# Maxout of a fused recurrent-attention and maxout-FFN kernel: evacuated by one ScalarE copy and two VectorE maxima of PSUM and SBUF

## The chip, the cores and the metric

One core of a Trainium2 chip. The metric is the device time of one execution in microseconds (us), the median of several. A run is called slow where it is over 1.5% above the fastest of its kernel, which here comes with a lower granted TensorE clock; ratios and verdicts use fast runs alone, while a median quoted without a further word is that of all runs, slow ones included. The profile's span is about 2 us shorter than the time, because it starts with the first recorded instruction. Engines: PE is TensorE, PEld its weight loads, DVE is VectorE, ACT is ScalarE, POOL is GpSimd, SP is the queue that issues the loads and stores.

## The reference, cut to what matters

```python
# attention: 4 batches, 8 heads, 768 positions, head size 48, a recurrence with decay alpha
state = alpha[:, :, t, :, None] * state + einsum('bhd,bhe->bhde', k[:, :, t], v[:, :, t])
y[:, :, t] = einsum('bhd,bhde->bhe', q[:, :, t], state)
# x: y as 3072 tokens x 384;  w1, w2, w3: 384 x 768;  w_out: 768 x 384
h = np.maximum(np.maximum(x @ w1, x @ w2), x @ w3)
out = h @ w_out
```

## The kernel before

The work is cut into 12 steps, each 128 positions of two batches (u = 0, 1). A step's pieces have one letter each, and hand-written strings fix in which order they are emitted; each engine runs its own part of that order strictly in turn. N takes logs of alpha, D multiplies by decays (matmul, two exponentials on ACT, then the k and q products), T transposes the products on PE and copies them out of PSUM, A makes and masks the scores, Y attends, X transposes y back into xT, M makes the decay factors of the state from D's third exponential, S updates the state, V scales v, G makes one gate tile, O projects. A gate pass has nine tiles: three groups of 256 columns by three weights. H is a run of matmuls on zeros that only keep PE's clock up. W casts a third of the gate weights (the last W: the output weights) on POOL. PSUM banks go round in rings: T, D and A share two banks ("w"), the gates have four.

```python
eng = nc.vector if s < 3 else nc.gpsimd
nc.gpsimd.tensor_mul(kv, raws[s, "k"][:, hs], ic)   # two SBUF inputs, fp32
eng.tensor_mul(qv, raws[s, "q"][:, hs], ac)
# ... T
nc.vector.tensor_copy(out=qkT, in_=tps)             # PSUM -> SBUF
# ... X
nc.vector.tensor_copy(out=xT.rearrange("p f u t -> p u f t"), in_=xtp_of.pop(s))
# ... gate: g is the weight (0, 1, 2), jg the group
if g < 2:
    h_of[g] = work.tile([P, 2, U * P], FP16, name=f"h{g}", tag=f"h{g}")
    nc.scalar.copy(out=h_of[g], in_=gps)
else:
    nc.vector.tensor_max(h_of[0], h_of[0], h_of[1])                             # two SBUF inputs
    nc.vector.tensor_max(hT_of[s][:, 2 * jg:2 * jg + 2, :], gps, h_of[0])       # PSUM and SBUF

STEADY = """T0 S0 N0 G0 G1 D0 T1 S1 O1 A0 G2 G3 O0 A1 G4 Y0 G5 Y1 X0 G6 D1 X1 G7 V0 G8 M0"""
```

## Time and profile before

| | before |
|---|---|
| median of 3 runs | 176.11 us |
| busy PE / DVE / ACT / POOL | 90% / 67% / 62% / 33% of a span of 174.4 us |
| one steady step (six of them alike) | 12.82 us, PE busy 12.04 |
| first gate matmul | at 31.34 us |
| PE waits for the copy qkT | 6 times, 4.7 us |

Read it from the engine that is never long without work. From the first gate matmul to the end PE is busy almost throughout, so a change pays only where it closes a hole of PE or lets the gates begin earlier. The lines that show this stand in the prediction below.

### The profile page before, as it was taken

Reading aid. Unit: us, or ns where it says so; the run is one execution under the profiler, and the core shown is the slowest. Engines: PE = TensorE matmul, PEld = TensorE weight load, DVE = VectorE, ACT = ScalarE, POOL = GpSimd, SP = SyncE. Lnnn points to the kernel's source line nnn. Section 1 sums busy time; section 2 is a strip of 40 time slices with the busy share of each in tenths; the row PEclk is TensorE's granted clock in tenths of the full one; section 3 lists DMA queues with packets and bytes.
Section 4 is the critical chain, followed back from the end, with each engine's and each line's share of the span. In section 5 each row is a group of like instructions: output and inputs, shape, how many; then the busy total and the mean of one; then the engine's idle time right before and its main releaser. Section 6 shows DMA issues by size and latency. Waiting matters only on the chain.

```text
span 174.4 us, 4372 instructions
## 1 busy us (share of the span) xinstructions
PE 156.9 (90%) x1762; PEld 120.2 (69%) x1762; DVE 116.1 (67%) x191; ACT 108.4 (62%) x205; POOL 57.1 (33%) x78
## 2 busy tenths in 40 slices
PE   7946788999999999989989999899899899899991
PEld 2324455799876777857867768778668768769870
DVE  4085769874646758588587687786777776776530
ACT  2627553466869775946946946946936937636551
POOL 0303128755191570540540540540540540500000
PEclk9995558999999999999999999999999999999999
DMA  6999999997999999998995955956951011011013
GB/s 132 220 218 218 170 243 325 358 347 157 180 230 219 180 294 213 222 218 200 218 217 117 225 125 116 204 137 136 182 137 51 0 45 49 0 49 45 0 49 135
DMA packets 107253, 28.70 MB, mean 165 GB/s; under 512 B 99809, under 2 KB 107233, under 8 KB 107233
## 3 DMA queue, kind: packets, MB, share of 16 engines
q1 hardware_dynamic: 106944, 28.32, 74.7%
q8 instruction: 14, 0.23, 0.6%
q10 hardware_dynamic: 288, 0.10, 0.3%
q14 instruction: 7, 0.05, 0.1%
HBM read 23.69 MB, written 4.72 MB: 163 GB/s over the span
## 4 chain that ended last, share of the span: by engine, by line
PE 78%; DVE 10%; ACT 4%; DMA 3%; issue 2%; SPq 1%; ACTq 0%; DVEq 0%
PE ops L282 14%; PE tps L179 6%; DVE qkT L183 4%; DVE lat L196 4%; DMA rq<-in_q_dram 3%; PE yps L210 2%; PE lps L146 2%; PE xtp L222 2%; PE yps L207 2%; PE wps L293 2%; PE sps L250 2%; PE sps L247 1%; SPq L85 1%; ACT xb L214 1%; PE lps L149 1%
## 5 line engine op out<-in xcount | busy, mean ns | idle before, releaser
L268 PEld LDWEIGHTS <-wcat 128*128 128x128 f16 x648 | 59.8, 98 | 8.7 <-issue 0.3
L282 PE MATMUL ops<-wo_97,hT 128*128 128x384 f16 x144 | 27.0, 326 | 0.6 <-DVE st_1_93 L254 0.6
L285 ACT COPY ob<-ops 128x384 f32<-128x384 f32 x24 | 11.6, 482 | 16.8 <-PE ops L282 16.8
L214 ACT ACTIVATE xb<-yps,c_69 128x384 f16<-128x384 f32 x24 | 14.0, 583 | 8.5 <-PE yps L210 8.4
L282 PEld LDWEIGHTS <-hT 128*128 128x128 f16 x144 | 13.6, 98 | 7.5 <-issue 0.7
L183 DVE COPY qkT<-tps 128x1024 f16<-128x1024 f16 x24 | 16.3, 686 | 2.6 <-PE tps L179 2.5
L155 ACT ACTIVATE ic<-lps,c_69 128x384 f32<-128x384 f32 x24 | 14.4, 599 | 2.3 <-PE lps L146 2.3
L156 ACT ACTIVATE ac<-lps,c_69 128x384 f32<-128x384 f32 x24 | 14.3, 597 | 0.0
L159 POOL TENSOR_TENSOR qk_86<-rk,ic 128x384 f16<-128x384 f32 x6 | 6.3, 1053 | 23.4 <-ACT ic L155 23.4
L193 PEld LDWEIGHTS <-qkT 48*128 48x128 f16 x192 | 6.1, 97 | 11.0 <-issue 7.5
L159 POOL TENSOR_TENSOR qk_85<-rk,ic 128x384 f16<-128x384 f32 x6 | 6.0, 998 | 22.3 <-ACT ic L155 16.4
L159 POOL TENSOR_TENSOR qk_87<-rk,ic 128x384 f16<-128x384 f32 x6 | 6.0, 1000 | 22.1 <-ACT ic L155 22.1
L159 POOL TENSOR_TENSOR qk_84<-rk,ic 128x384 f16<-128x384 f32 x6 | 6.0, 1001 | 20.8 <-ACT ic L155 20.8
L210 PE MATMUL yps<-vt,lat 128*128 128x48 f16 x192 | 11.8, 188 | 0.1
L170 ACT ACTIVATE vt<-rv,c_69 128x768 f16<-128x768 f32 x12 | 11.5, 957 | 0.0
L225 DVE COPY xT<-xtp 128x768 f16<-128x768 f16 x12 | 6.7, 556 | 7.0 <-PE xtp L222 7.0
L293 PE MATMUL wps<-blank 128*128 128x512 f16 x26 | 10.2, 553 | 1.2 <-DVE blank L340 1.2
L210 PEld LDWEIGHTS <-lat 128*128 128x128 f16 x192 | 10.2, 100 | 0.7 <-DVE lat L196 0.3
L222 PE MATMUL xtp<-c_68,xb 128*128 128x128 f16 x72 | 8.4, 228 | 1.0 <-ACT xb L214 0.8
L207 PEld LDWEIGHTS <-qkT 128*128 128x128 f16 x80 | 7.6, 96 | 0.2
L293 PEld LDWEIGHTS <-blank 128*128 128x128 f16 x26 | 3.1, 130 | 5.2 <-issue 3.3
L179 PE MATMUL tps<-c_68,qk_85 128*128 128x128 f16 x48 | 4.5, 248 | 2.3 <-DVE qkT L183 1.6
(442 smaller groups left out, 376.1 us busy)
## 6 DMA issues: line engine op xcount, KB each, us to landing
ra<-in_alpha_dram SPq DMA_DIRECT2D x12, 384.0 KB, 4.6
rk<-in_k_dram SPq DMA_DIRECT2D x12, 384.0 KB, 5.6
rq<-in_q_dram SPq DMA_DIRECT2D x12, 384.0 KB, 5.9
rv<-in_v_dram SPq DMA_DIRECT2D x12, 384.0 KB, 5.8
out_dram<-ob SPq DMA_DIRECT2D x24, 192.0 KB, 2.1
ws_0_114<-in_moe_w_dram SPq DMA_DIRECT2D x1, 384.0 KB, 5.2
ws_1_116<-in_moe_w_dram SPq DMA_DIRECT2D x1, 384.0 KB, 4.7
ws_2_118<-in_moe_w_dram SPq DMA_DIRECT2D x1, 384.0 KB, 5.6
```

What stands on the lines that cost most here:

```text
L155: nc.scalar.activation(out=ic, in_=lv, func=AFT.Exp, bias=nat_c, scale=-1.0)
L156: nc.scalar.activation(out=ac, in_=lv, func=AFT.Exp, bias=at_c)
L159: nc.gpsimd.tensor_mul(kv, raws[s, "k"][:, hs], ic)
L179: nc.tensor.transpose(tps[:, i, p, :], qk[:, i, u * HP + p].rearrange("p a b -> p (a b)"), ident)
L183: nc.vector.tensor_copy(out=qkT, in_=tps)
L210: nc.tensor.matmul(yps[:, p, i, :], lat[:, i, p, :], vt[:, u * H + 2 * p + i, :], start=(cb == 0), stop=(cb == 0 or i == 1))
L214: nc.scalar.mul(xb, yps.rearrange("p a b d -> p (a b d)"), ys_c)
L222: nc.tensor.transpose(xtp[:, u, f, :], xb[:, f * P:(f + 1) * P], ident)
L268: nc.tensor.matmul(gps[:, j, :], wcat[:, f, g, jj * P:(jj + 1) * P], xT[:, f].rearrange("p u t -> p (u t)"), start=(f == 0), stop=(f == NF ...
L282: nc.tensor.matmul(ops, hT_of[s][:, jj, u * P:(u + 1) * P], wo16[:, jj, :], start=(jj == 0), stop=(jj == NJ - 1))
L285: nc.scalar.copy(out=ob, in_=ops)
L293: nc.tensor.matmul(wps, blank[:, :P], blank, start=True, stop=True)
```

## The change

The intent: leave VectorE no instruction with two SBUF inputs in the steady part, so that it cannot collide there with GpSimd's products. ScalarE copies only the first of three gate tiles, VectorE takes two maxima of a PSUM tile and an SBUF tile, ScalarE takes over the copy of xT, and in the opening (the first three steps) the k product goes to VectorE. The order strings were set anew.

```diff
-        nc.gpsimd.tensor_mul(kv, raws[s, "k"][:, hs], ic)
+        eng.tensor_mul(kv, raws[s, "k"][:, hs], ic)
...
-            nc.vector.tensor_copy(out=xT.rearrange("p f u t -> p u f t"), in_=xtp_of.pop(s))
+            nc.scalar.copy(out=xT.rearrange("p f u t -> p u f t"), in_=xtp_of.pop(s))
...
-            h_of[g] = work.tile([P, 2, U * P], FP16, name=f"h{g}", tag=f"h{g}")
-            nc.scalar.copy(out=h_of[g], in_=gps)
+            h = work.tile([P, 2, U * P], FP16, name=f"h{g}", tag=f"h{g}")
         else:
-            nc.vector.tensor_max(h_of[0], h_of[0], h_of[1])
-            nc.vector.tensor_max(hT_of[s][:, 2 * jg:2 * jg + 2, :], gps, h_of[0])
+            h = hT_of[s][:, 2 * jg:2 * jg + 2, :]
+        if g == 0:
+            nc.scalar.copy(out=h, in_=gps)
+        else:
+            nc.vector.tensor_max(h, gps, h_of[g - 1])
+        h_of[g] = h
...
     PROLOGUE: (cut)  H8 -> H9; H5 ahead of T0@2 gone (H0); W0 from behind S1@0 to ahead of D0@2
-    STEADY = """T0 S0 N0 G0 G1 D0 T1 S1 O1 A0 G2 G3 O0 A1 G4 Y0 G5 Y1 X0 G6 D1 X1 G7 V0 G8 M0"""
+    STEADY = """N0 T0 S0 T1 G0 G1 D0 S1 O1 A0 O0 G2 A1 G3 Y0 G4 D1 G5 Y1 G6 X0 X1 G7 M0 V0 G8"""
     (cut: FIRST, SECOND and LAST are reordered too)
```

More of the change, by code (lines that the diff above doesn't have):

```diff
@@ L321, in emit @@
                 fn(step, int(piece[1:]))
-    PROLOGUE = """N0@0 H11@0 D0@0 D1@0 N0@1 H8@0 V0@0 T0@0 T1@0 A0@0 A1@0 D0@1 Y0@0 D1@1 X0@0 Y1@0
-        T0@1 H2@0 A0@1 T1@1 N0@2 V0@1 A1@1 X1@0 Y0@1 D0@2 D1@2 X0@1 H5@0 T0@2 Y1@1 M0@0 T1@2
-        S0@0 V0@2 A0@2 S1@0 W0 X1@1 A1@2 W1 W2 W3"""
-    FIRST = """G0@0 G1@0 G2@0 G0@1 G1@1 G2@1 Y0@2 G3@0 G4@0 G5@0 G3@1 G4@1 Y1@2 X0@2 G5@1 G6@0 G7@0
+    PROLOGUE = """N0@0 H11@0 D0@0 D1@0 H9@0 N0@1 V0@0 T0@0 T1@0 A0@0 A1@0 D0@1 Y0@0 D1@1 T0@1 N0@2
+        H2@0 X0@0 A0@1 Y1@0 T1@1 V0@1 Y0@1 A1@1 X1@0 X0@1 W0 D0@2 D1@2 T0@2 Y1@1 T1@2 X1@1
+        H0@0 A0@2 V0@2 M0@0 S0@0 S1@0 W1 W2 A1@2 W3"""
+    FIRST = """G0@0 G1@0 Y0@2 G2@0 G0@1 G1@1 G2@1 G3@0 G4@0 X0@2 G5@0 G3@1 G4@1 G5@1 G6@0 G7@0 Y1@2
         G8@0 G6@1 X1@2 G7@1 G8@1"""
-    SECOND = """N0@3 G0 G1 G2 D0@3 D1@3 M0@1 G3 G4 O0@0 G5 T0 O1@0 G6 N0 S0 O0@1 A0 V0@3 G7 T1 D0 S1
-        O1@1 A1 G8 Y0 Y1 D1 M0 X0 V0 X1"""
-    STEADY = """T0 S0 N0 G0 G1 D0 T1 S1 O1 A0 G2 G3 O0 A1 G4 Y0 G5 Y1 X0 G6 D1 X1 G7 V0 G8 M0"""
-    LAST = """G0 G1 G2 G3 G4 G5 O0 G6 G7 G8 O1"""
+    SECOND = """N0@3 G0 G1 G2 D0@3 D1@3 G3 O0@0 N0 G4 G5 T0 G6 M0@1 V0@3 S0 O1@0 A0 O0@1 G7 T1 D0 S1
+        O1@1 A1 Y0 D1 Y1 X0 M0 G8 X1 V0"""
+    STEADY = """N0 T0 S0 T1 G0 G1 D0 S1 O1 A0 O0 G2 A1 G3 Y0 G4 D1 G5 Y1 G6 X0 X1 G7 M0 V0 G8"""
+    LAST = """G0 G1 G2 G3 G4 G5 G6 G7 O1 G8 O0"""
     load(1)
```

## The prediction

> **What bounds the kernel now.** I read the page's busy shares first (PE 90%, DVE 67%, ACT 62%, POOL 33%), then the busy time of each engine stretch by stretch, then the waits of PE, and last the instructions in order of time around one wait. The loop's steps repeat every 12.82 us, so I cut the stretches at the steps (each starts at the first transposes of a step). The columns: stretch, its length, then busy us (and instructions) of PE, PEld, DVE, ACT, POOL; granted clock; DMA share; GB/s.
>
> ```profile
> 59.58:71.97 12.39, 12.28 (x154) 9.88 (x152) 8.05 (x14) 9.25 (x20) 4.95 (x7) 1.00 0.94 215
> 84.79:97.61 12.82, 12.04 (x151) 9.63 (x149) 9.46 (x15) 8.77 (x18) 4.47 (x7) 1.00 0.88 186
> 136.07:148.90 12.83, 12.05 (x152) 9.65 (x150) 9.45 (x15) 8.78 (x18) 4.49 (x7) 1.00 0.09 32
> 148.90:160.40 11.50, 10.87 (x134) 8.61 (x132) 9.36 (x15) 6.07 (x11) 1.86 (x4) 1.00 0.10 36
> ```
>
> PE works 12.04 us of each 12.82, at full clock and whatever the DMA does (share 0.88 or 0.09, same step). PE is the bound, with one hole of 0.78 us a step. The waits of PE name the hole (us in total, times, longest); from 35 to 60 us and from 160 us on PE waits for nothing:
>
> ```profile
> PE tps L179 <- DVE qkT L183: 4.7, 6, 0.8
> PE ops L282 <- DVE st_1_93 L254: 0.6, 1, 0.6
> ```
>
> The hole in order of time (start, duration, what):
>
> ```profile
> 119.90 0.43 DVE L275 TENSOR_TENSOR h_2102<-h_2102,h_2134 128x512 f16<-128x512 f16 x1
> ...
> 122.59 1.00 POOL L159 TENSOR_TENSOR qk_85<-rk,ic 128x384 f16<-128x384 f32 x1 [6.84 <-ACT ic L155]
> 123.55 1.01 POOL L160 TENSOR_TENSOR qk_85<-rq,ac 128x384 f16<-128x384 f32 x1
> 123.57 1.27 DVE L275 TENSOR_TENSOR h_2186<-h_2186,h_2218 128x512 f16<-128x512 f16 x1 [1.03 <-ACT h_2218 L273]
> 124.94 0.69 DVE L276 TENSOR_TENSOR hT<-gps_2222,h_2186 128x512 f16<-128x512 f32 x1
> 125.55 0.68 DVE L183 COPY qkT<-tps 128x1024 f16<-128x1024 f16 x1
> 126.28 0.61 PE L179 MATMUL tps<-c_68,qk_85 128*128 128x128 f16 x8 [0.78 <-DVE qkT L183]
> ```
>
> The same maximum of two SBUF tiles takes 0.43 us at 119.90, with POOL idle, and 1.27 us at 123.57, beside a POOL product that runs until 124.56: 0.84 us too much. The maximum of PSUM and SBUF behind it starts late, the copy of the transposes starts late, and PE's second group of transposes waits for that copy (it needs the bank) 0.78 us. So the hole is the lock, carried through three VectorE instructions.
>
> **What the Trainium skill says.** "SBUF — State Buffer", section "SBUF: two separate sides": VectorE and GpSimd share a port pair under an exclusive lock; an instruction of VectorE with two SBUF inputs takes part against a GpSimd one that reads SBUF, and the loser blocks for the whole instruction. The trace agrees (0.43 against 1.27 us). "TensorE: Matmul & The Clock Gate", Part 1: the array's clock is halved until an activity window of about 3.4 us was busy. The trace agrees in the opening: eight transposes took 1.01 us at 20.49 and 0.45 us from start to next from 27.9 on. "VectorE: DVE Perf Modes", section "The perf-mode tier table": an elementwise VectorE instruction of two tensors gets 2x for 16-bit SBUF operands and 1x with a PSUM operand. The trace agrees: 0.42 against 0.69 us for 512 columns.
>
> **The change part by part.**
>
> 1. Maxout. Before, per group of three gate tiles: two ScalarE copies (587 ns) and, on VectorE, 0.42 us (SBUF with SBUF) and 0.69 us (PSUM with SBUF). After: one copy and two of 0.69 us. Three groups a step. ScalarE: 3 x 0.59 = 1.8 us less. VectorE: 3 x (0.69 - 0.42) = 0.8 us more, minus the 0.84 us of lock.
>
> 2. The copy of xT goes from VectorE (0.56 us) to ScalarE. Estimate for 768 columns on ScalarE: the copies took 482 ns for 384 and 587 for 512 columns, 0.82 ns a column, so 482 + 384 x 0.82 = 0.80 us. ScalarE ends at about 8.8 - 1.8 + 0.8 = 7.8 us a step, VectorE at 9.45 + 0.8 - 0.84 - 0.56 = 8.9 us. Neither nears 12.04.
>
> 3. No VectorE instruction of the steady part has two SBUF inputs any more, so the lock has nothing to meet. POOL is as before.
>
> 4. New orders. I walked one steady step with the durations above, PE being in order: T 0.44, S 0.34, T 0.44, two gates of 0.66, D 0.16, S 0.34, O 0.97, A 0.43, O 0.97, and so on. The tight places: the first A needs the exponentials of D out of its bank. D starts at 2.53, its result is there at 2.9, the two exponentials end at 3.97, A's second bank is asked for at 4.0: just in time. The second A (6.06) needs the second masked product of the first one (ends about 5.7). X1 (10.40) needs the scaled copy that ends at about 10.35. The second T needs T1's bank, free since D1's exponentials (9.6 of the step before). No hole is left, but three margins are under 0.4 us; I charge 0.05 us a step. Steps 4 to 9: 6 x 0.78 = 4.7 us. Step 10: the 0.63 us wait for the state (its stretch shows 11.50 - 10.87). Step 3 (12.39 against 12.04): 0.3 us. Together 5.6, minus 8 x 0.05 = 0.4: **5.2 us gained** between 59 and 160 us.
>
> 5. The opening. For the first three steps the k product goes to VectorE too. Two products together took 2.25 us on both engines when they locked each other (25.33 to 27.58), and four in a row on VectorE at 0.65 us are 2.6 us, but the first pair is ready after 1.3. Followed through the opening's chain (products, transposes, copy, scores, mask, twice per step) this makes each of the three rounds 0.4 to 0.6 us later on VectorE, not cumulatively, because the next round waits for its own data and banks. Five warming matmuls (2.34 us at 25.07) are gone just ahead of the third round, and the clock had come back in them; without them PE may be at half clock until 30 or 34 us. The gates began at 31.34; from there PE was busy without a hole up to 60. By my walk they begin at 31.9 to 32.6, with up to 2 us of gates at half clock. Against that, the counts of warming matmuls were plainly set with care (9 and 0 where 8 and 5 stood), so I take less than the walk: **1.2 us lost**. The weights don't bind: their last cast ended at 38.95, and the gates that need it came at 41.5.
>
> 6. The second step's order puts the last scores, two attends and D1 close together: an attend comes about 1.2 us after scores whose two masked products need about 1.5. I charge **0.4 us lost**. The last step and the tail (18 output matmuls, one copy, one DMA) are as before: 0.
>
> Sum: -5.2 + 1.2 + 0.4 = -3.6. From 176.1: **172.5**; I lean a little further, to **172.3**, since the skipped holes in the opening (PE was busy 26.9 of the first 35 us) leave room for the reordering to win something.
>
> **The rivals.**
>
> A. Nothing fills: another wait takes the hole's place. For it: VectorE stays at 8.9 of 12 us in strict order, and margins of 0.03 to 0.4 us stand at the scores and at X1. Against it: VectorE and ScalarE both lose work, and the walk finds no wait above 0.1 us. If half the hole comes back (0.4 us a step), the time is 175.
>
> B. The clock in the opening. For it: granted clock 0.5 in the slices from 13 to 26 us, and the gap where the five matmuls stood. Against it: other pieces moved forward into 20 to 24 us, which may wake the clock earlier, and then 2.34 us of dummy work is simply gone. If it stays low until 37 us: 175. If it wakes early: 170.5.
>
> C. ScalarE becomes the bound. For it: xT, which all gates of the next step need, now stands in its queue behind a gate copy. Against it: 7.8 us of work in 12, and between X1 and the next gates stand two gates, two transposes and one update (2.5 us) against 1.3 us for the copy with its wait. I give it no weight; it would make 176.
>
> **Range and chances.** Full steady gain with a neutral opening is 170.6; steady gain with a cold opening is 174 to 175; half the steady gain with a cold opening is 176.5. So 169.8 to 174.8 for 8 in 10. Faster by over 2% is below 172.6, nearly at my centre: 0.56. Within 2%: 0.42. Slower by over 2% (above 179.6) would take both rivals and more: 0.02.
>
> **What would show it right or wrong.** Right: steps of 12.0 to 12.1 us with PE busy 12.04; no wait of PE for the qkT copy; every steady maximum at 0.69 us; xT on ScalarE at about 0.80 us; POOL's products still at 1.00 us. Step 5: the start of the first gate matmul (31.34 before) and whether its six take 0.66 or 1.3 us. Step 6: waits of PE between 55 and 62 us. It would be wrong if PE showed a new wait in each step (for a masked product, an exponential or xT), or if gates began later than 33 us.

## The result, and the profile after

The changed kernel took 170.83 us (median of 4 fast runs, 170.35 to 171.68), the kernel before 176.22 us in the same count of runs (one of them slow; 176.11 us over its three fast ones). The ratio of the fast runs is 0.9712, 95% interval 0.9656 to 0.9767: faster by 2.9%. Ratios here are the mean time of one kernel's fast runs over that of the other's fast runs of the same rounds, so not quite the ratio of the medians quoted.

The busy time by steps in the kernel after, cut as before (stretch, length, then busy us of PE, PEld, DVE, ACT, POOL; clock; DMA share; GB/s); the rows are step 3, two steady steps, and most of step 10:

```profile
60.41:72.46 12.05, 12.05 (x152) 9.67 (x149) 8.08 (x14) 9.23 (x17) 5.27 (x9) 1.00 1.05 236
84.39:96.32 11.93, 11.93 (x151) 9.64 (x149) 8.76 (x15) 8.11 (x16) 4.28 (x6) 1.00 1.03 215
96.32:108.25 11.93, 11.93 (x152) 9.64 (x149) 8.76 (x15) 8.10 (x16) 4.28 (x6) 1.00 0.82 168
144.28:155.00 10.72, 10.72 (x134) 8.65 (x132) 8.21 (x14) 4.62 (x9) 0.00 (x0) 1.00 0.11 38
```

The reader is to see that length and PE busy are now equal: there is no hole. VectorE went from 9.46 to 8.76 us and ScalarE from 8.77 to 8.10 us a step. The end of one steady step, in order of time (start, duration, what):

```profile
104.62 0.69 DVE L278 TENSOR_TENSOR h_1882<-gps_1875,h_1858 128x512 f16<-128x512 f32 x1 [0.30 <-ACT xb L214]
105.57 0.69 DVE L278 TENSOR_TENSOR hT<-gps_1902,h_1882 128x512 f16<-128x512 f32 x1 [0.26 <-PE gps_1902 L268]
105.61 1.00 POOL L159 TENSOR_TENSOR qk_84<-rk,ic 128x384 f16<-128x384 f32 x1 [3.88 <-ACT ic L155]
106.57 0.99 POOL L160 TENSOR_TENSOR qk_84<-rq,ac 128x384 f16<-128x384 f32 x1
107.08 0.81 ACT L225 COPY xT<-xtp 128x768 f16<-128x768 f16 x1
107.71 0.69 DVE L278 TENSOR_TENSOR h_1950<-gps_1943,h_1932 128x512 f16<-128x512 f32 x1 [1.45 <-PE gps_1943 L268]
```

VectorE's maximum at 105.57 runs beside POOL's product at 105.61, and both take what they take alone. The copy of xT takes 0.81 us on ScalarE.

The opening moved the other way in part. The first gates in the kernel after:

```profile
30.51 1.46 PE L268 MATMUL gps_514<-xT,wcat 128*128 128x256 f16 x6
31.76 1.49 PE L268 MATMUL gps_523<-xT,wcat 128*128 128x256 f16 x6
...
33.72 0.84 PE L268 MATMUL gps_547<-xT,wcat 128*128 128x256 f16 x6
```

Six matmuls take 1.46 and 1.49 us at first and 0.84 later: the first two gates ran at about half the later rate. (A row's duration contains the tail of its last matmul, which overlaps the next row; from start to start it is 1.25 and 1.28 us against 0.66.)

Where the 5.6 us of span (174.4 to 168.8) came from, as differences of starts of the same pieces in the two traces:

| part | before | after | difference |
|---|---|---|---|
| start to first gate matmul | 31.34 | 30.51 | -0.83 |
| first gate to the third pass's first gate | 13.12 (to 44.46) | 14.47 (to 44.98) | +1.35 |
| from there to step 3's transposes | 15.12 (to 59.58) | 15.27 (to 60.25) | +0.15 |
| step 3 | 12.23 (to 71.81) | 12.04 (to 72.29) | -0.19 |
| steps 4 to 9 | 76.92 (to 148.73) | 71.82 (to 144.11) | -5.10 |
| step 10 | 12.16 (to 160.89) | 11.38 (to 155.49) | -0.78 |
| step 11 and tail | 13.51 | 13.31 | -0.20 |

(The stretches of the busy tables are cut at starts as the chain of work gives them, up to 0.2 us later than the instruction's own row, which is used here. The prediction's first stretch mixed the two, so step 3 was 12.23 us, not 12.39.)

### The profile page after: what moved, and what is told of

Same layout as the page of the kernel before. It is cut to its first block, busy times and chain, and to the rows that moved or that the text cites. A ratio compares the mean times of both kernels' runs of the same rounds, so it can differ in the third digit from the quotient of the medians.

```text
span 168.8 us, 4329 instructions
## 1 busy us (share of the span) xinstructions
PE 156.9 (93%) x1758; PEld 121.1 (72%) x1758; DVE 112.2 (66%) x185; ACT 99.0 (59%) x181; POOL 49.0 (29%) x72
## 4 chain that ended last, share of the span: by engine, by line
PE 81%; SPq 7%; DMA 3%; ACT 3%; DVE 2%; issue 1%; ACTq 0%
PE ops L285 14%; SPq L85 7%; PE tps L179 6%; DMA ra<-in_alpha_dram 3%; PE yps L210 3%; PE xtp L222 2%; PE lps L146 2%; PE yps L207 2%; PE sps L250 2%; PE sps L247 2%; DVE lat L196 1%; PE lps L149 1%; ACT xb L214 1%; PE gps_514 L268 1%; PE gps_523 L268 1%
## 5 line engine op out<-in xcount | busy, mean ns | idle before, releaser
L155 ACT ACTIVATE ic<-lps,c_69 128x384 f32<-128x384 f32 x24 | 13.9, 581 | 8.4 <-PE lps L146 5.1
L285 PEld LDWEIGHTS <-hT 128*128 128x128 f16 x144 | 12.8, 98 | 7.5
L156 ACT ACTIVATE ac<-lps,c_69 128x384 f32<-128x384 f32 x24 | 13.8, 575 | 0.0
L159 POOL TENSOR_TENSOR qk_87<-rk,ic 128x384 f16<-128x384 f32 x6 | 6.0, 997 | 21.9 <-ACT ic L155 21.9
L225 ACT COPY xT<-xtp 128x768 f16<-128x768 f16 x12 | 9.6, 803 | 1.0 <-PE xtp L222 1.0
L296 PE MATMUL wps<-blank 128*128 128x512 f16 x22 | 8.0, 528 | 1.2 <-DVE blank L343 1.2
L159 POOL TENSOR_TENSOR qk_86<-rk,ic 128x384 f16<-128x384 f32 x4 | 4.0, 997 | 15.4 <-ACT ic L155 15.4
L130 POOL CAST wcat<-ws_0_114 128x768 f16<-128x768 f32 x1 | 0.8, 823 | 26.3 <-DMA ws_0_114<-in_moe_w_dram 26.3
L159 POOL TENSOR_TENSOR qk_85<-rk,ic 128x384 f16<-128x384 f32 x4 | 4.0, 995 | 13.9 <-ACT ic L155 13.9
L222 PE MATMUL xtp<-c_68,xb 128*128 128x128 f16 x72 | 7.4, 228 | 0.5 <-ACT xb L214 0.3
L159 POOL TENSOR_TENSOR qk_84<-rk,ic 128x384 f16<-128x384 f32 x4 | 4.0, 996 | 12.4 <-ACT ic L155 12.4
L222 PEld LDWEIGHTS <-xb 128*128 128x128 f16 x72 | 5.2, 101 | 2.3 <-ACT xb L214 0.9
```

Source lines behind the costliest of these rows:

```text
L155: nc.scalar.activation(out=ic, in_=lv, func=AFT.Exp, bias=nat_c, scale=-1.0)
L156: nc.scalar.activation(out=ac, in_=lv, func=AFT.Exp, bias=at_c)
L159: eng.tensor_mul(kv, raws[s, "k"][:, hs], ic)
L222: nc.tensor.transpose(xtp[:, u, f, :], xb[:, f * P:(f + 1) * P], ident)
L285: nc.tensor.matmul(ops, hT_of[s][:, jj, u * P:(u + 1) * P], wo16[:, jj, :], start=(jj == 0), stop=(jj == NJ - 1))
```

## The experiments

The theory: the gain is that of one VectorE instruction a step, the third group's maximum of two SBUF tiles, which loses the shared port to POOL and delays the copy that PE waits for. The first rival: the gain comes from the work taken off ScalarE and VectorE in sum. The second: it comes from the new orders. For the opening: the clock is what the new one loses. All kernels below gave correct results.

**The third group alone, and the other two alone.** Everything as before except which groups of the maxout are done the new way.

```diff
         if g < 2:
             h_of[g] = work.tile(...)
-            nc.scalar.copy(out=h_of[g], in_=gps)
+        if g == 0:
+            nc.scalar.copy(out=h_of[0], in_=gps)
+        elif g == 1 and jg == 2:          # the complement: jg < 2
+            nc.vector.tensor_max(h_of[1], gps, h_of[0])
+        elif g == 1:
+            nc.scalar.copy(out=h_of[1], in_=gps)
+        elif jg == 2:                     # the complement: jg < 2
+            nc.vector.tensor_max(hT_of[s][:, 2 * jg:2 * jg + 2, :], gps, h_of[1])
         else:                             # as before
```

> The kernel before with one part of the change: only the third maxout group of each gate pass (the one whose two-SBUF maximum took 1.27 us in the steady steps) is done as one copy and two maxima of PSUM and SBUF; the other two groups, the orders, xT on VectorE and k on POOL stay. Lock theory (the hole of PE comes from that one instruction blocked by POOL's product): the wait of PE for the qkT copy goes, steps fall from 12.82 to about 11.95 us, the wait of the tenth step goes too, total about 170.3 us. Load theory (the gain comes from work taken off ScalarE and VectorE in sum): a third of the maxout's relief, so about 174.5 us, hole about 0.5 us.

> The complement: only the first two groups are done the new way, the third keeps its maximum of two SBUF tiles. Lock theory: the 1.27 us instruction and the wait of PE stay, steps 12.82 us, total 175.7 to 176.3 us. Load theory: two thirds of the relief, total about 172.5 us.

Measured: the third group alone 169.19 us (ratio 0.9625, 0.9583 to 0.9666), the other two alone 175.91 us (ratio 0.9994, 0.9972 to 1.0016). The third group alone is the whole gain (the changed kernel's ratio is 0.9712), its trace has no wait of PE between 60 and 160 us, and two thirds of the relief are worth nothing. In the kernel with the third group alone, the end of a step reads:

```profile
95.06 1.00 POOL L159 TENSOR_TENSOR qk<-rk,ic 128x384 f16<-128x384 f32 x1 [5.95 <-ACT ic L155]
95.17 0.69 DVE L276 TENSOR_TENSOR h<-gps,h 128x512 f16<-128x512 f32 x1 [0.17 <-PE gps L268]
95.97 0.69 DVE L280 TENSOR_TENSOR hT<-gps,h 128x512 f16<-128x512 f32 x1
96.02 1.01 POOL L160 TENSOR_TENSOR qk<-rq,ac 128x384 f16<-128x384 f32 x1
96.58 0.68 DVE L183 COPY qkT<-tps 128x1024 f16<-128x1024 f16 x1
```

POOL works beside both maxima and neither grows: they have one SBUF input each. The copy qkT begins 1.02 us after the step's transposes (95.56), where before it began 2.46 us after them (125.55 against 123.09). In the complement the old picture stands:

```profile
110.83 1.01 POOL L160 TENSOR_TENSOR qk<-rq,ac 128x384 f16<-128x384 f32 x1
110.85 1.27 DVE L282 TENSOR_TENSOR h<-h,h 128x512 f16<-128x512 f16 x1 [1.03 <-ACT h L278]
...
113.56 0.61 PE L179 MATMUL tps<-c,qk 128*128 128x128 f16 x8 [0.78 <-DVE qkT L183]
```

**D1 moved, nothing else.** The lock needs the two instructions at the same time, so moving POOL's products must do what changing VectorE's instruction does.

```diff
-    STEADY = """... G4 Y0 G5 Y1 X0 G6 D1 X1 G7 V0 G8 M0"""
+    STEADY = """... G4 Y0 D1 G5 Y1 X0 G6 X1 G7 V0 G8 M0"""
```

> The kernel before with nothing but one piece moved in the steady order: D1 (which releases POOL's second pair of products) stands before the sixth gate instead of before the eighth. No engine changes. Lock theory: POOL's products end about 2 us before the third maximum of two SBUF tiles, which then takes 0.42 us; the wait of PE for the qkT copy goes; steps 11.9 to 12.1 us, total 170 to 171.5 us. Theory that an instruction with two SBUF inputs is costly whatever stands beside it: it stays 1.27 us and the total 176 us.

Measured: 171.66 us (171.63 over its three fast runs; ratio 0.9749, 0.9711 to 0.9787), just above the expected range. Its profiled run was a slow one (173.85 us), but the stretch shown had the full clock. In it the third group's maximum takes its 0.42 us again:

```profile
97.05 1.00 POOL L160 TENSOR_TENSOR qk<-rq,ac 128x384 f16<-128x384 f32 x1
...
98.79 0.42 DVE L275 TENSOR_TENSOR h<-h,h 128x512 f16<-128x512 f16 x1 [0.77 <-ACT h L273]
```

So the same instruction with two SBUF inputs is cheap when POOL has ended (here 0.74 us earlier, not the expected 2 us), and PE's wait for the copy qkT is gone. The steps came out at 12.17 us, above the expected 11.9 to 12.1: D1's exponentials now stand ahead of the second scaled copy on ScalarE, and PE's weight loads for X1 waited 0.4 us for that copy. X1 started 0.31 us late for it, about the 0.29 us by which these steps are longer than those of the third group alone (11.88).

One thing neither edit holds still: in the kernel before, the third maximum had also waited 1.03 us for ScalarE's copy h_2218, which stands behind D1's exponentials, and both edits loosen that wait too (with the third group alone its second maximum reads PSUM and needs no such copy). The traces part the two for the moved D1. Counted from the step's first transposes, the maximum began after 0.48 us before (123.09 to 123.57) and after 0.22 us here (98.57 to 98.79), and the copy qkT after 2.46 us and 1.35 us. Of the 1.11 us, then, 0.26 is the earlier start and 0.85 the maximum's duration. An estimate from these: with the duration alone mended, 0.84 us of the hole (0.93 us from starts, see below) would have gone and about 0.1 us stayed. No run here takes the lock away and nothing else.

**Orders alone, and engines alone.** The first has the new strings with the old operations (old maxout, xT on VectorE, k on POOL), the second the new operations with the old strings.

> The new orders with the old engines (maxout with the two-SBUF maximum, xT on VectorE, k on POOL in the opening). Lock theory: the orders move POOL's second pair of products away from the end of the step (D1 stands before the sixth gate instead of before the eighth), so the lock may strike elsewhere or not at all: if the steps come out near 12.0 us the order alone dodges it; I expect 12.0 to 12.4 us and a total of 171 to 174 us. Load theory: with old engines most of the gain is gone, about 175 us.

> The old orders with the new engines (maxout of one copy and two maxima, xT on ScalarE, k on VectorE in the opening). Lock theory: no lock, so no hole: steps about 11.95 us; the opening loses up to 1 us to k on VectorE with the old order; total 170.5 to 171.5 us. Rival that the orders carry the gain: steps stay above 12.4 us, total above 173.5 us.

Measured: engines alone 171.09 us (ratio 0.9736, 0.9704 to 0.9768). Orders alone was told unclear at 180.27 us (ratio 1.018, 1.0095 to 1.0265; its fast runs were 177.94 and 179.83 us). The new engines gain with the old strings, and the new strings do not gain with the old engines; for the total of the orders alone my expectation of 171 to 174 us missed. Inside the steady part I was right about the lock: in the steps that I read, every maximum of two SBUF tiles took 0.42 or 0.43 us, because D1 stands earlier in the new string, and a step took 12.34 us. What I had missed is the opening. In the new string W0 stands ahead of D0@2, and POOL works strictly in order:

```profile
29.33 0.83 POOL L130 CAST wcat<-ws 128x768 f16<-128x768 f32 x1 [0.28 <-DMA ws<-in_moe_w_dram]
30.12 1.95 POOL L159 TENSOR_TENSOR qk<-rk,ic 128x384 f16<-128x384 f32 x2
```

The k products of the third round wait behind casts that wait for the weights, and PE waited 4.5 us for them, once; its first two gates, from 36.13 us, then ran at half rate as well. Part of its 12.34 us a step is in the trace: two gate copies (1.30 us at 93.55) stand ahead of D0's exponentials on ScalarE, and the scores that need their bank take 0.66 us (at 95.57) where the changed kernel's take 0.40 (at 88.33). The rest I did not follow. In the changed kernel k's products don't queue behind the casts, so W0 can stand early; no run has the new orders with only k back on POOL. Engines alone shows the reverse need: with the old strings, xT on ScalarE cost one wait of 1.4 us of PE (gates for the copy xT, at 62.14 us), because in that queue it stood behind three exponentials and the scaling of v. Why its steps took 12.06 us is open.

**xT back on VectorE.** The changed kernel with one line undone.

```diff
-            nc.scalar.copy(out=xT.rearrange("p f u t -> p u f t"), in_=xtp_of.pop(s))
+            nc.vector.tensor_copy(out=xT.rearrange("p f u t -> p u f t"), in_=xtp_of.pop(s))
```

> The changed kernel with the copy of xT back on VectorE (0.56 us there, 0.80 us on ScalarE). If the move to ScalarE matters (VectorE too loaded with six maxima of 0.69 us), a hole of some tenths of a us a step appears at the second transposes, total 172 to 174 us. If it doesn't, 170.5 to 171 us. VectorE has 8.8 us of 11.9 now, so I expect the second.

Measured: 170.68 us (ratio 0.9709), the same as the changed kernel's 0.9712. VectorE is busy 9.31 us of steps of 11.93 us and nothing waits for it. The move of xT is worth nothing in the new orders.

**The clock in the opening.** Two warming matmuls more, where PE idled 0.79 us in the changed kernel.

```diff
-        ... D0@2 D1@2 T0@2 Y1@1 ...
+        ... D0@2 D1@2 H2@0 T0@2 Y1@1 ...
```

> The changed kernel with two warming matmuls set between D1 and the transposes of the third opening round, where PE now idles about 0.8 us. Clock theory (the first two gates take 1.39 and 1.28 us because the array runs at half clock until about 33 us): the clock is full from about 27 us, the first two gates take 0.66 us each, the gates of the next steps begin 1.0 to 1.4 us earlier, total 169.4 to 169.9 us. Rival: these gates are slow for another reason (weights, banks): nothing changes, 170.8 us or slightly more.

Measured: 169.38 us (ratio 0.9632, 0.9609 to 0.9656). The first two gates now run at full rate. Start to start the twelve matmuls of the row take about 1.3 us where they took 2.5 us:

```profile
25.56 1.03 PE L179 MATMUL tps<-c,qk 128*128 128x128 f16 x8
26.74 1.03 PE L179 MATMUL tps<-c,qk 128*128 128x128 f16 x8
27.65 0.50 PE L222 MATMUL xtp<-c,xb 128*128 128x128 f16 x3
...
30.75 1.48 PE L268 MATMUL gps<-xT,wcat 128*128 128x256 f16 x12
```

The transposes ahead are still at half rate (1.03 us for eight). By the granted clock it came back at about 29.1 us, later than the 27 that I expected, but before the gates.

One trace, however, is not enough to read the clock from. Up to D1@2 the two kernels are the same program, and yet the first line below, of the changed kernel, is at full rate and the third, of the kernel with two matmuls more, at half:

```profile
20.40 0.61 PE L179 MATMUL tps<-c_68,qk_85 128*128 128x128 f16 x8 [0.35 <-DVE lat L196]
23.66 0.48 PE L146 MATMUL lps<-la_82,c_68 128*128 128x384 f16 x1 [0.28 <-DVE lat L196]
...
20.14 1.01 PE L179 MATMUL tps<-c,qk 128*128 128x128 f16 x8 [0.35 <-DVE lat L196]
```

In the changed kernel's trace the granted clock was full from about 20.1 to 23.5 us, was lost before the idle stretch that I had blamed (24.3 to 25.1), and came back at about 33.8; in the trace of xT back on VectorE, with the same opening strings, it stayed at half until about 35.2. What carries the conclusion is the set: without the two matmuls the first two gates ran at half rate in both of these traces, with them at full rate in all three (this one and both of the combined kernel below), and the fast runs of this kernel don't overlap those of the two without (169.11 to 169.48 us against 169.65 to 171.68). So warming there pays about 1.4 us; that the idle stretch is what lost the clock is not shown.

**The parts that won, together.** The third group's maxout alone on the kernel before, with the changed kernel's PROLOGUE and FIRST strings, k on VectorE in the opening, and the two warming matmuls.

> The kernel before with only the third maxout group changed, put together with the changed kernel's opening and first-pass orders (k on VectorE there) and the two warming matmuls. If the gains add (steps of 11.88 us as in the kernel with the third group alone, an opening 0.8 to 1.3 us shorter), 167.8 to 168.6 us; if the opening's gain is taken by the next wait, 169.2 us.

Measured: 168.92 us (ratio 0.961, 0.9591 to 0.9629), with steps of 11.88 us. Its gates began at 30.91 us at full rate. The time is just above the expected range of 167.8 to 168.6, and clear of the changed kernel (0.9656 to 0.9767).

A second look set it beside the third group alone, and added the third group alone with k on VectorE in the opening (old strings), all of one chip:

> The kernel before with only the third maxout group changed, and k on VectorE in the opening, everything else as before. Lock theory for the opening: the products of a round no longer block each other (0.56 us each on VectorE alone, against 1.0 us on POOL and up to 1.14 on VectorE when both run), but four stand in one queue, so the first transposes of a round come earlier and the second a little later: within 0.5 us of the same kernel with k on POOL. Theory that moving k is itself a gain of the change: 0.8 us faster or more.

> The kernel before with only the third maxout group changed, a second time, beside the combined one: about 169.2 us. If the combined kernel's opening is worth what it gained in the changed kernel (1.4 us by warming), this one is 0.8 us or more slower; its own opening is warm already, so I expect 0.2 to 0.6 us.

> The combined kernel (third group alone, changed opening with two warming matmuls) a second time: about 168.9 us, 0.2 to 0.6 us faster than the third group alone.

Measured: 169.65, 169.82 and 169.23 us (over the fast runs alone 169.65, 169.37 and 169.16; two of six were slow in each of the last two), ratios 0.9549, 0.9534 and 0.9555, with intervals that cover each other (0.9493 to 0.9604, 0.9468 to 0.96, 0.9476 to 0.9635). This chip was less steady; the kernel before ran from 175.63 to 179.05 us on it. So the three are not told apart: no gain of 0.8 us from the move of k is seen, and an advantage of the combined kernel over the third group alone is not shown.

## Why the prediction was right

The predicted 172.3 us (169.8 to 174.8) stood against 170.83 us measured; the direction and the range held, and the centre was 1.5 us too slow. The errors all lie on one side and don't cancel: in the span of the two profiled executions they are 0.9 us in the steady part, 0.7 in the opening, 0.25 in the second step and 0.2 in the tail, less the 0.2 us that it leaned: 1.8 us there, 1.5 in the medians. By its steps:

1. **Maxout.** Right in its durations: 0.69 us for every steady maximum read, and VectorE at 8.76 us where 8.9 was worked out. But of the three groups only the third mattered, as the pair of experiments showed. The other two are in the change for nothing.
2. **xT to ScalarE.** The estimate of 0.80 us was measured as 803 ns in the mean of twelve. ScalarE stood at 8.1 where 7.8 was worked out. The experiment showed that this move pays nothing in the new orders.
3. **The lock.** Right, and shown from two sides: by another VectorE instruction at the same time as POOL, and by the same instruction at another time. It left out one smaller part, the maximum's wait for ScalarE's copy (0.26 us of the delay, above).
4. **The steady gain.** Mechanism right, size too small: 5.2 us predicted, 6.1 us measured (0.19 + 5.10 + 0.78). The mis-sized term is the hole. The listed 0.78 us counts from the modelled end of the matmul before it. D's matmul starts at 112.36 and the transposes start at 113.46 in the step before the one shown, 1.10 us apart, where without a wait the next piece starts 0.17 us after D (98.69 to 98.86 in the kernel after). The real hole is 0.93 us, and the step fell by 0.89. So "PE busy 12.04" was no floor. The wait for the state in step 10, 0.63 us, stood behind the same 1.27 us maximum (at 149.21) and went with it. And the 0.05 us a step charged for the tight margins was not needed in five of the six steps 4 to 9; one of them took 12.15 us, and why is open.
5. **The opening.** 1.2 us lost was predicted, 0.52 measured (-0.83 + 1.35), but by other parts than the walk said. The gates began earlier, not later (30.51, predicted 31.9 to 32.6). The step that failed is "each of the three rounds 0.4 to 0.6 us later on VectorE": I had taken 0.65 us for a product from starts that lay partly beside POOL's, while alone on VectorE it took 0.56 us, and 0.47 from start to start. Moving k alone bears this out: on one chip, and with the clock half in nearly the same stretches, the gates began at 30.87 us with k on VectorE and at 30.99 with k on POOL. Some of the 0.83 us is luck of the clock: with the same opening strings and no stretch of full clock at 20 us, the kernel with xT back began its gates at 31.10. The second term, gates at half clock, was real: the first two gates alone lost 1.22 us (2.53 from start to start against 1.31) of the 1.35, and with two warming matmuls more it was gone. My argument that the counts of warming matmuls had been set with care pointed the wrong way here.
6. **The second step.** 0.4 us lost was predicted, 0.15 measured. The trace has the wait that was named, for a masked product (0.27 us, ahead of the matmul at 57.82), and one of 0.35 us for the scaled copy (at 60.07); I did not test it. The tail was called 0 and gained 0.20.

Of the rivals, A (a new wait takes the place of the old) did not come in the changed kernel; it did come in the kernel with D1 moved, at X1. B came in its first form, half clock at the gates, but to about 33.8 us and not 37. C was not seen in the changed kernel; with the old strings (engines alone) its fear came true once, as 1.4 us of waiting for xT.

One reading of the prediction compares unlike things: eight transposes at 1.01 us is a duration, 0.45 us is from start to next. Like with like, from start to next, it is 0.82 us (17.18 to 18.00) against 0.44 (59.58 to 60.02); the conclusion, about half rate, stands.

## What to carry to other kernels

Look for one instruction kind with two durations in the same trace: the longer one can point to a collision, and following what starts late behind it tells whether it reaches the bounding engine. Then change that instance alone: here a slower instruction (0.69 for 0.42 us) that was not blocked was the faster choice, and an earlier partner on the other engine gained about two thirds as much (2.5% against 3.75%). When the opening is reordered, read the rate of the first repeated matmuls again, in more than one execution, because the warming may have to be set again with it.

## What the Trainium skill lacked or had wrong

- "SBUF — State Buffer", "SBUF: two separate sides": the lock and its condition are as the runs show (0.42 to 0.43 us free, 1.27 us beside POOL's product; 0.69 us unchanged for the form with one PSUM input). The page says, under "Who interferes with whom", that an instruction with at most one SBUF input does not contend; it does not spell out that reading one operand from PSUM gets there and can pay although the form is slower, nor that two durations of one form give the lock away.
- "TensorE: Matmul & The Clock Gate", Part 1: it doesn't say how busy a window must be. Here an opening with an idle stretch of 0.79 us in front of the third round's transposes was at half clock until about 33.8 us in one trace and about 35.2 in another, and with two matmuls in that place it was at full rate at its gates in three traces (from 29.76, 30.75 and 30.91 us).
- "ScalarE: Activation LUTs", "What ACT_TABLE_LOAD costs": 186 ns + 0.833 ns a column for immediate scale and bias gives an estimate of 826 ns for 768 columns; the copies from PSUM took 803 ns in the mean, and 587 for 512 columns (613 by the page). The slope agrees, the fixed part is about 25 ns smaller.
- No page found says that the idle time listed ahead of a matmul is counted from a modelled end and so understates the hole: 0.78 us listed, 0.93 us from starts.
